# First batch's token mixing in plain float32 on unsplit operands, and channel weights split in two chains

## The chip, the cores and the metric

One core of a Trainium2 chip runs the whole kernel: TensorE (PE for its matmuls, PEld for its weight loads), VectorE (DVE), ScalarE (ACT), GpSimd (POOL), SyncE (SP, which issues most of the DMAs), on-chip memory (SBUF), the matmul accumulators (PSUM, eight banks) and device memory. The metric is device microseconds of one execution of the kernel; lower is better. A number of executions of each kernel gives a median; one more was recorded by the hardware profiler, and every duration in this document comes from such a recording.

## The reference

The inputs are q, k and v (8 batches, 8 heads, 576 positions, 64 wide), two weights of a token mixer (`w_tok1` 576x256, `w_tok2` 256x576) and two of a channel mixer (`w_ch1` 512x1536, `w_ch2` 1536x512). The weights are float64 in memory. Cut to what matters:

```python
q_d, k_d, v_d = means of q, k, v over groups of 4 positions
out = repeat(softmax_attention(q_d, k_d, v_d), 4) + local_attention(q, k, v, |i - j| < 4)
x = out as (batch, 576, 512)
h = relu(x.T @ w_tok1) @ w_tok2          # token mixing, over positions
u = x + h.T
h2 = relu(u @ w_ch1) @ w_ch2             # channel mixing, over the 512 channels
return u + h2
```

## The kernel before, in words

**Batches.** Each of the 8 batches b goes through attention, token mixing (`mix`), and channel mixing (`first`, `second`). Attention works in four head pairs (`pooled`, four steps over the pooled positions: sd, td, ad and their softmax) and five position tiles t of 128, 128, 128, 128 and 64 rows (`local`: scores sc, softmax on DVE and ACT, transpose pT, its copy pt on ACT, product av, copy to x on ACT at L536; the last tile's x is named x_last).

**Token mixing.** `splits` makes two rounded parts of each x tile, a float32r copy on ACT (L570) and the remainder on DVE (L572), in a tile xh. `products` multiplies them, for five tiles into one accumulator named t1 (in the profile it is "t<-xh,W"); each product is `mm3` (L116): three float32r matmuls, high by high, high by low, low by high. `takes` makes relu of it in the same two parts (ACT L607, DVE L609, tile hid), for each of two halves f in turn. Then eight groups t2, for two position chunks (256 and 320 columns) and four channel blocks c: transposes of x through an identity (L595) and two `mm3` with hid ("t<-W,hid"). `takes` copies each group to u (ACT L620) and takes its largest absolute value (DVE L622). `scaled` brings the largest value of a chunk to all partitions (`everywhere`: DVE L544, PE L547, DVE L550, PE L553), and makes uh, u scaled in two float16 parts (ACT L639, DVE L641).

**Channel mixing.** `first` is 12 blocks f for each chunk, each 12 float16 matmuls on uh and the first weight (in the profile "c<-uh,CW"), followed by relu in two parts (L725, L727). `second` is 12 matmuls for each quarter of its sum, on h and the second weight ("c<-h,CX").

**Weights.** Each weight piece comes as float64 words, and `to_f32` makes float32 of it in three steps: ACT (L203), POOL (L206), DVE (L208). The nine token pieces (five of W1, four of W2, tiles W_raw) are then split into two float32r parts by `token_weight`: ACT L226, DVE L228. The channel weights C1 and C2 (12 tiles of 128x512 each) get column norms on PE (L293, L312), a scale, one for each four tiles of C1 and one for all of C2, and a split into two float16 parts by `parts`: ACT L280, DVE L282. The parts of tile i are written over place i, and its float32 lies in place i+1, so tile i+1 can be split only after tile i. `scale` does this in one generator, so the 12 splits run one after the other.

**Order of work.** Each piece of work is a generator that yields `step(engine, estimated us, needs, take, give)`. Until the first batch's channel mixing is through, `drive` plays these estimates as a clock per engine, and issues the step that can start first; among those of the same engine within 0.15 us of it, the one whose generator stands first in the list goes first. The list is a string of group letters, `"LWUMTSaCDPHmQAh"`: loads L, token weights W, up-steps U, mixing of batch 0 M, C2's scale and splits T, C1's scale and splits S, attention of batch 1 a, conversion of C1 C and of C2 D, c1 and c2 products P and Q, the load of batch 1 H, its mixing m, attention of batch 0 A, batch 2's load h. What `drive` chooses is fixed when the program is made; on the chip every engine runs its queue in that order and waits at each instruction for what it needs. Where the estimate leaves PE idle before the first batch's scaled values, `keep_busy` puts matmuls on a tile of ones (L153, "busy<-junk"). After that the remaining work is laid into the channel products of batches 1 to 7 by `side` and `tick`, not by `drive`.

Of the kernel before, what the change touches and what calls it, by code (L numbers as in the profile page):

```python
# [29 lines left out]
PATIENCE = 0.15  # L30
ORDER = """p0+p1 p0 p1 p0 p1 l0+l1 l0 l1 p0 p0 p1 p1 l0 l1 l0 l1 p0 p0 p1 p1 l0 l0 l1 l1
# [5 lines left out]
def tile_ups_attention_mixer(ctx, tc, qk, vw, vr, w1, w2, c1, c2, out):  # L37
# [182 lines left out]
    def token_weight(i, n, f):  # L220
        yield step("A", 0.0, ("W", "raw", i))
        raw = made["W", "raw"][i]
        yield from to_f32(raw, made["W", "raw", i])
        y = raw.rearrange("p (n two) -> p n two", two=2)[:, :, 0].bitcast(F32)
        yield step("A", 0.1 + n * 0.0011)
        nc.scalar.copy(f[:, 0], y)  # L226
        e = yield step("V", 0.08 + n * 0.0012)
        nc.vector.tensor_tensor(f[:, 1], y, f[:, 0].bitcast(F32), ALU.subtract)  # L228
        make(("W", "y", i), e)
        make(("W", "read", i), e)  # L230

# [12 lines left out]
    class Channel:  # L244
# [3 lines left out]
        def __init__(self, name):  # L248
            self.name, self.fin, self.banks = name, [], {}
            self.mx = sb.tile([128, NQ], F32, name=f"{name}_mx")  # L250
            self.inv = [sb.tile([128, 1], F32, name=f"{name}_inv{q}") for q in range(NQ)]
            self.s = [sb.tile([128, 1], F32, name=f"{name}_s{q}") for q in range(NQ)]

        def tile(self, i, *needs):
            name = self.name
            yield step("A", 0.0, (name, "raw", i))
            raw = made[name, "raw"][i]
            e = yield from to_f32(raw, made[name, "raw", i], lambda: self.place[i + 1].bitcast(U32), *needs)
# [3 lines left out]
            self.sums(i, self.place[i + 1].bitcast(BF16).rearrange("p (n two) -> p n two", two=2)[:, :, 1])  # L262
# [13 lines left out]
        def parts(self, i):  # L276
            y = self.place[i + 1]
            f = self.place[i].bitcast(F16).rearrange("p (a n) -> p a n", a=2)
            yield step("A", 0.72)
            nc.scalar.activation(f[:, 0], y, AF.Copy, scale=self.s[i // 4])  # L280
            t = yield step("V", 0.75)
            nc.vector.scalar_tensor_tensor(f[:, 1], y, self.s[i // 4], f[:, 0], ALU.mult, ALU.subtract)  # L282
            self.fin.append(f)
            make((self.name, i), t)

    class First(Channel):
# [8 lines left out]
        def scale(self):  # L295
            for q in range(NQ):
                yield from self.norms(q)
                big = yield from everywhere(f"C1_n{q}", self.mx[:, q:q + 1])
                e = yield step("V", 0.45, give="g")

                self.root(big, 2.0 ** (4.5 + 0.5 - 8), self.inv[q], self.s[q])
                make(("C1", "scale", q), e)
                for i in range(4 * q, 4 * q + 4):
                    yield from self.parts(i)

    class Second(Channel):
# [8 lines left out]
        def scale(self):  # L315
# [5 lines left out]
            yield step("V", 0.9, give="g")  # L321
# [4 lines left out]
            for i in range(NF):  # L326
                yield from self.parts(i)
# [18 lines left out]
    C1.place = singles(NF + 1, "CW")  # L346
# [7 lines left out]
    W2 = [sb.tile([128, 2, S], F32R, name=f"W2_{k}") for k in range(2)]  # L354
    W1_PIECES = [(u32(w1[s0:s0 + n]), 256) for s0, n in TILES]
# [200 lines left out]
    def mix(st):  # L556
# [8 lines left out]
        def splits():  # L565
            for t in range(NT):
# [8 lines left out]
        def products():  # L575
            for t in range(NT):
                e = yield step("P", 1.5, ("W", "y", t), ("xh", b, t), take="" if t else f"gg>{b}")
                if t == 0:
                    st.acc = P2(f"t1_{b}")
                for f in range(2):  # L580
                    mm3(st.acc[:, f], lambda a: W1[t][:, a, 128 * f:128 * f + 128], lambda a: st.xh[t][:, a],
                        t == 0, t == NT - 1)
                make(("t1", b, t), e)
            for ch in range(2):
                s0, N = CHUNKS[ch]
                for c in range(4):
                    e = yield step("P", 1.2, ("W", "y", NT + 3), ("hid", b),
# [15 lines left out]
        def takes():  # L603
            for f in range(2):
# [7 lines left out]
            for ch in range(2):  # L612
# [3 lines left out]
                for c in range(4):  # L616
                    yield step("A", 0.4, ("t2", b, ch, c))
# [87 lines left out]
    def first(st, ch, places):  # L705
        b, N = st.b, CHUNKS[ch][1]
        hs = st.h[ch] = []
        for f in range(NF):
            e = yield step("P", 12 * N * 0.43e-3, ("C1", f), ("uh", b, ch),
                           *([("mixed", b)] if places[f // 3] != "h" else []), take=f"m>1{ch}")  # L710
            uh = st.uh[ch]
            ps = PM(f"c1_{b}_{ch}_{f}")[:, :N]
            for c in range(4):
                mm3(ps, lambda a: C1.fin[f][:, a, 128 * c:128 * c + 128], lambda a: uh[c][:, a], c == 0, c == 3)
# [54 lines left out]
    def second_weights():  # L769
        yield step("S", 0.0, *(("C1", "read", i) for i in range(NF)))  # L770
        C2.place = pairs("CX") + singles(1, "CY")
# [24 lines left out]
    with tc.manual_schedule():  # L796
# [14 lines left out]
        group["T"] = [second_weights()]  # L811
# [7 lines left out]
        streams = [x for k in "LWUMTSaCDPHmQAh" for x in group[k]]  # L819
        left = drive(streams, [("over", 0, 1)] + [("uh", 1, 0)] * (B > 1))  # L820
# [107 lines left out]
```

## Time and profile before

| | |
|---|---|
| median of 3 runs | 945.24 us (937.5 to 946.85) |
| the profiled execution, its own time | 938.98 us |
| its span, first to last instruction | 937.1 us |
| mean granted TensorE clock | 0.985 |
| TensorE in it | 11407 matmul instructions |
| DMA | 68.29 MB, mean 73 GB/s |

Times in the views are us from the span's start. A row of the timeline has start, duration, engine, line, operation, output<-inputs, shape, count, and in brackets the idle time before it with the one it waited for. A row of the groups has the same, then the busy time in all and the mean of one in ns, then idle time before. "t<-xh,W", "t<-W,hid" are the token products; "c<-uh,CW" and "c<-h,CX" the channel products. A busy PE also counts the matmuls on ones.

### The profile page before, as it was taken

Reading aid. Unit: us, or ns where it says so; the run is one execution under the profiler, and the core shown is the slowest. Engines: PE = TensorE matmul, PEld = TensorE weight load, DVE = VectorE, ACT = ScalarE, POOL = GpSimd, SP = SyncE. Lnnn points to the kernel's source line nnn. Section 1 sums busy time; section 2 is a strip of 40 time slices with the busy share of each in tenths; the row PEclk is TensorE's granted clock in tenths of the full one; section 3 lists DMA queues with packets and bytes.
Section 4 is the critical chain, followed back from the end, with each engine's and each line's share of the span. In section 5 each row is a group of like instructions: output and inputs, shape, how many; then the busy total and the mean of one; then the engine's idle time right before and its main releaser. Section 6 shows DMA issues by size and latency. Waiting matters only on the chain.

```text
span 937.1 us, 25758 instructions
## 1 busy us (share of the span) xinstructions
PE 894.0 (95%) x11407; PEld 709.8 (76%) x11413; DVE 482.5 (51%) x1174; ACT 297.7 (32%) x627; POOL 117.0 (12%) x191
## 2 busy tenths in 40 slices
PE   6779998999999999999989999999999999999998
PEld 3556877778867787787867788777977878777876
DVE  6788995437552565327552375426653275333221
ACT  2476553124141332314232241423323142422120
POOL 6350410120310003000130002200030000000000
PEclk9888999999999999999999999999999999999999
DMA  8772432510440006300170004400062000000000
GB/s 238 251 290 99 145 65 66 162 53 2 132 121 8 23 4 191 60 15 16 49 203 3 22 9 145 108 8 23 2 198 54 16 16 20 20 1 29 13 12 29
DMA packets 28222, 68.29 MB, mean 73 GB/s; under 512 B 3504, under 2 KB 14000, under 8 KB 26864
## 3 DMA queue, kind: packets, MB, share of 16 engines
q1 hardware_dynamic: 25552, 64.30, 23.2%
q10 hardware_dynamic: 2560, 2.36, 0.9%
q8 instruction: 89, 1.46, 0.7%
q14 instruction: 21, 0.17, 0.1%
HBM read 54.85 MB, written 9.44 MB: 69 GB/s over the span
## 4 chain that ended last, share of the span: by engine, by line
PE 72%; DMA 5%; DVE 3%; ACT 2%; issue 1%; SPq 0%; ACTq 0%
PE c L116 50%; PE t L116 10%; DMA qk<-in_qk_dram 4%; PE ad L463 3%; PE sc L495 2%; PE t L595 2%; PE av L531 1%; PE sd L436 1%; PE td L454 1%; DMA vw<-od 1%; PE pT L518 1%; ACT x L536 1%; DVE uh L641 1%; PE um_b L553 0%; SPq L371 0%
## 5 line engine op out<-in xcount | busy, mean ns | idle before, releaser
L116 PE MATMUL c<-uh,CW 128*128 128x256 f16 (+1 forms) x2304 | 306.4, 287 | 2.3 <-DVE u L753 1.8
L116 PE MATMUL c<-h,CX 128*128 128x256 f16 (+1 forms) x2304 | 304.5, 287 | 0.1
L116 PEld LDWEIGHTS <-CW 128*128 128x128 f16 x2304 | 219.0, 98 | 68.6 <-issue 14.7
L116 PEld LDWEIGHTS <-CX 128*128 128x128 f16 x2304 | 218.1, 98 | 58.2 <-issue 1.6
L727 DVE SCALAR_TENSOR_TENSOR h<-c,h 128x256 f16<-128x256 f32 (+1 forms) x192 | 86.7, 452 | 135.0 <-ACT h L725 134.9
L725 ACT ACTIVATE h<-c 128x256 f16<-128x256 f32 (+1 forms) x192 | 77.7, 406 | 181.4 <-PE c L116 178.3
L400 POOL TENSOR_TENSOR vr<-vr 72x256 f32<-72x256 f32 x64 | 53.0, 830 | 496.0 <-DMA vr<-in_vr_dram 494.5
L753 DVE SCALAR_TENSOR_TENSOR u<-c,io,u 128x256 f32<-128x256 f32 (+1 forms) x64 | 32.9, 514 | 100.0 <-PE c L116 100.0
L622 DVE TENSOR_REDUCE umx<-t 128x1 f32<-128x256 f32 (+1 forms) x64 | 29.2, 457 | 84.7 <-ACT u L620 76.2
L116 PE MATMUL t<-xh,W 128*128 128x512 f32 x240 | 68.9, 423 | 1.2 <-ACT x L536 1.2
L620 ACT COPY u<-t 128x256 f32<-128x256 f32 (+1 forms) x64 | 25.5, 398 | 133.3 <-PE t L116 110.5
L116 PE MATMUL t<-W,hid 128*128 128x256 f32 (+1 forms) x384 | 66.7, 308 | 0.0
L116 PEld LDWEIGHTS t<-W,hid 128*128 128x128 f32 x384 | 53.2, 189 | 0.3 <-DVE hid L609 0.3
L536 ACT COPY x<-av 128x512 f32<-128x512 f32 x32 | 18.6, 583 | 109.6 <-PE av L531 38.1
L116 PEld LDWEIGHTS t<-xh,W 128*128 128x128 f32 x240 | 44.1, 194 | 11.4 <-ACT x L536 2.0
L463 PE MATMUL ad<-vd,ptd 72*72 72x65 f32 x512 | 39.0, 229 | 7.5 <-issue 6.6
L463 PEld LDWEIGHTS ad<-vd,ptd 72*72 72x72 f32 x512 | 37.3, 146 | 8.9 <-issue 7.6
L531 PE MATMUL av<-vw,pt 47*32 47x64 f32 x2304 | 34.0, 228 | 9.5 <-DMA vw<-od 5.8
L531 PEld LDWEIGHTS av<-vw,pt 47*32 47x32 f32 x2304 | 27.7, 107 | 18.2 <-issue 5.8
L422 DVE TENSOR_REDUCE qd<-qk 128x72 f32<-128x288 f32 x64 | 25.9, 446 | 27.7 <-DMA qk<-in_qk_dram 27.6
L639 ACT ACTIVATE uh<-u,us 128x256 f16<-128x256 f32 (+1 forms) x64 | 29.7, 524 | 26.9 <-DVE us L122 19.8
L495 PEld LDWEIGHTS sc<-qk 64*32 64x32 f32 x2304 | 23.8, 105 | 12.2 <-issue 10.0
(108 smaller groups left out, 841.4 us busy)
## 6 DMA issues: line engine op xcount, KB each, us to landing
qk<-in_qk_dram SPq DMA_DIRECT2D x32, 579.0 KB
vw<-in_vw_dram SPq DMA_DIRECT2D x32, 351.0 KB
vr<-in_vr_dram SPq DMA_DIRECT2D x64, 144.0 KB
C_raw<-in_c_dram SPq DMA_DIRECT2D x16, 512.0 KB
out_dram<-u SPq DMA_DIRECT2D x32, 160.0 KB
C_raws<-in_c_dram SPq DMA_DIRECT2D x8, 512.0 KB
out_dram<-u SPq DMA_DIRECT2D x32, 128.0 KB
vw<-od ACTq DMA_DIRECT2D x32, 72.0 KB
```

Of the source, the lines that this page charges most:

```text
L116: nc.tensor.matmul(ps, lhs(a), rhs(c), start=first and i == 0, stop=last and i == 2, **kw)
L400: nc.gpsimd.tensor_add(t[:, 0:2], t[:, 0:2], t[:, 2:4])
L422: nc.vector.tensor_reduce(o, q[:, h], axis=AX.X, op=ALU.add)
L463: nc.tensor.matmul(ps[:, g, par], pt[:, par, kg, G * g:G * g + G], st.vd[:, kg, 2 * pr + par], start=kg == 0, stop=kg == 1)
L495: nc.tensor.matmul(ps[QB * j:QB * j + QB, par, WB * hp:WB * hp + WB], st.qk[hp][p, QB * g:QB * g + QB], st.qk[hp][p, S + QB * g:S + QB * g ...
L531: nc.tensor.matmul(ps[QB * j:QB * j + QB, par, D * hp:D * hp + D], pt[p, hp, QB * j:QB * j + QB], st.vw[h][p, g, D * hp:D * hp + D], start ...
L536: nc.scalar.copy(x[:n].rearrange("p hp two d -> p two hp d"), ps[:n, :, :4 * D].rearrange("p two (hp d) -> p two hp d", hp=4))
L622: nc.vector.tensor_reduce(umx[ch][:, c:c + 1], ps, axis=AX.X, op=ALU.max, apply_absolute_value=True)
L639: nc.scalar.activation(t[:, 0], st.u[ch][c], AF.Copy, scale=s)
L725: nc.scalar.activation(ht[:, 0], ps, AF.Relu)
L727: nc.vector.scalar_tensor_tensor(ht[:, 1], ps, 0.0, ht[:, 0], ALU.max, ALU.subtract)
L753: nc.vector.scalar_tensor_tensor(us[c], banks[c], io, us[c], ALU.mult, ALU.add)
```

## The change

For batch 0 alone, the token products take x, W1, relu and W2 unsplit, in plain float32: one `matmul` call in place of the three of `mm3`. `splits` runs from batch 1 on, and `takes` of batch 0 has the two ACT relus and no DVE step. The float32 of W1 goes to a tile of its own in the u1 buffers (W1_y), that of W2 to a new tile W2_y. The two-part split of the nine pieces, which batches 1 to 7 use, is a generator `token_split` in a new group w, next to last in the list; it needs the first batch's t1 product of that tile (W1) or all of its token products (W2). A copy of batch 0's u waits for the first of these splits, and one of batch 1's for all five of W1, since u1 is shared.

The float32 of C1 and C2 now lies two places up (i+2), so the splits go in two chains, even and odd tiles, in generators of their own (`split(0)`, `split(1)`; group E for C1, in T for C2). The planner's list becomes `"LWUMSETaCDPHmQAwh"`: S and E stand before T. The planner's estimate of a t1 tile of batch 0 is 1.8 instead of 1.5 us.

```diff
+PRIORITY = "LWUMSETaCDPHmQAwh"
...
     def token_weight(i, n, f):
...
-        yield from to_f32(raw, made["W", "raw", i])
-        y = raw.rearrange("p (n two) -> p n two", two=2)[:, :, 0].bitcast(F32)
-        yield step("A", 0.1 + n * 0.0011)
-        nc.scalar.copy(f[:, 0], y)
-        e = yield step("V", 0.08 + n * 0.0012)
-        nc.vector.tensor_tensor(f[:, 1], y, f[:, 0].bitcast(F32), ALU.subtract)
+        if i < len(TILES):
+            y = WY[i] = T([f.shape[0], n], F32, "u1", f"W1_y{i}")
+        else:
+            y = WY[i]
+        e = yield from to_f32(raw, made["W", "raw", i], lambda: u32(y))
         make(("W", "y", i), e)
         make(("W", "read", i), e)
+
+    def token_split(i, n, f):
+        yield step("A", 0.1 + n * 0.0011, ("W", "y", i), ("t1", 0, i) if i < len(TILES) else ("mixed", 0))
+        nc.scalar.copy(f[:, 0], WY[i])
+        e = yield step("V", 0.08 + n * 0.0012)
+        nc.vector.tensor_tensor(f[:, 1], WY[i], f[:, 0].bitcast(F32), ALU.subtract)
+        make(("W", "split", i), e)
...
         def parts(self, i):
-            y = self.place[i + 1]
+            y = self.place[i + 2]
...
-                for i in range(4 * q, 4 * q + 4):
-                    yield from self.parts(i)
+
+        def split(self, k):
+            for i in range(k, NF, 2):
+                yield step("A", 0.0, ("C1", "scale", i // 4))
+                yield from self.parts(i)
...
-            for i in range(NF):
+            make(("C2", "scale"), made["S2"])
+
+        def split(self, k):
+            yield step("A", 0.0, ("C2", "scale"))
+            for i in range(k, NF, 2):
                 yield from self.parts(i)
...
-            for t in range(NT):
+            for t in range(NT if b else 0):
                 yield step("A", 0.62, ("x", b, t), *([("over", 0, 0)] if b == 1 else []),
...
-                    mm3(st.acc[:, f], lambda a: W1[t][:, a, 128 * f:128 * f + 128], lambda a: st.xh[t][:, a],
-                        t == 0, t == NT - 1)
+                    if b == 0:
+                        n = TILES[t][1]
+                        nc.tensor.matmul(st.acc[:, f], WY[t][:, 128 * f:128 * f + 128], xf(t)[:n],
+                                         start=t == 0, stop=t == NT - 1)
+                    else:
+                        mm3(st.acc[:, f], lambda a: W1[t][:, a, 128 * f:128 * f + 128], lambda a: st.xh[t][:, a],
+                            t == 0, t == NT - 1)
...
-                        mm3(ps, lambda a: st.hid[k][:, a, 128 * c:128 * c + 128],
-                            lambda a: W2[k][:, a, s0:s0 + N], False, k == 1, skip_group_check=True)
+                        if b == 0:
+                            nc.tensor.matmul(ps, st.hid[k][:, 128 * c:128 * c + 128], W2_y[:, k, s0:s0 + N],
+                                             start=False, stop=k == 1, skip_group_check=True)
+                        else:
+                            mm3(ps, lambda a: st.hid[k][:, a, 128 * c:128 * c + 128],
+                                lambda a: W2[k][:, a, s0:s0 + N], False, k == 1, skip_group_check=True)
...
+            if b == 0:
+                ht = T([128, 2, 512], F32, "xh", "hid0")
+                for f in range(2):
+                    e = yield step("A", 0.6, ("t1", 0, NT - 1), give="gg>0" if f else "")
+                    nc.scalar.activation(ht[:, f], st.acc[:, f], AF.Relu)
+                    st.hid.append(ht[:, f])
+            for f in range(2 if b else 0):
...
+                    yield step("A", 0.4, ("t2", b, ch, c), *[("W", "split", i) for i in range(NT if b else 1) if b < 2 and ch and c == (0 if b else 3)])
...
+        group["w"] = [token_split(i, pieces[i][1], fin[i]) for i in range(len(pieces))]
+        group["E"] = [C1.split(k) for k in range(2)]
+        group["T"] = [second_weights(), C2.split(0), C2.split(1)]
```

More of the change, by code (lines that the diff above doesn't have):

```diff
@@ L248, in __init__ @@
         def __init__(self, name):
-            self.name, self.fin, self.banks = name, [], {}
+            self.name, self.fin, self.banks = name, {}, {}
             self.mx = sb.tile([128, NQ], F32, name=f"{name}_mx")
@@ L257, in tile @@
             raw = made[name, "raw"][i]
-            e = yield from to_f32(raw, made[name, "raw", i], lambda: self.place[i + 1].bitcast(U32), *needs)
+            e = yield from to_f32(raw, made[name, "raw", i], lambda: self.place[i + 2].bitcast(U32), *needs)
             make((name, "read", i), e)
@@ L261, in tile @@
             make((name, "y", i), e)
-            self.sums(i, self.place[i + 1].bitcast(BF16).rearrange("p (n two) -> p n two", two=2)[:, :, 1])
+            self.sums(i, self.place[i + 2].bitcast(BF16).rearrange("p (n two) -> p n two", two=2)[:, :, 1])
         def norms(self, q):
@@ L282, in parts @@
             nc.vector.scalar_tensor_tensor(f[:, 1], y, self.s[i // 4], f[:, 0], ALU.mult, ALU.subtract)
-            self.fin.append(f)
+            self.fin[i] = f
             make((self.name, i), t)
@@ L320, in scale @@
             big = yield from everywhere("C2_n", self.mx)
-            yield step("V", 0.9, give="g")
+            made["S2"] = yield step("V", 0.9, give="g")
             self.root(big, 2.0 ** (4.5 + 2 + 0.5 - 14), ic, self.s[0])
@@ L345, in tile_ups_attention_mixer @@
     C1, C2 = First("C1"), Second("C2")
-    C1.place = singles(NF + 1, "CW")
+    C1.place = singles(NF + 2, "CW")
     ic = sb.tile([128, 1], F32, name="ic")
@@ L354, in tile_ups_attention_mixer @@
     W2 = [sb.tile([128, 2, S], F32R, name=f"W2_{k}") for k in range(2)]
+    W2_y = sb.tile([128, 2, S], F32, name="W2_y")
+    WY = {len(TILES) + 2 * k + j: W2_y[:, k, HS * j:HS * j + HS] for k in range(2) for j in range(2)}
     W1_PIECES = [(u32(w1[s0:s0 + n]), 256) for s0, n in TILES]
@@ L576, in products @@
             for t in range(NT):
-                e = yield step("P", 1.5, ("W", "y", t), ("xh", b, t), take="" if t else f"gg>{b}")
+                e = yield step("P", 1.5 if b else 1.8, *([("W", "split", t), ("xh", b, t)] if b else [("W", "y", t), ("x", 0, t)]),
+                               take="" if t else f"gg>{b}")
                 if t == 0:
@@ L586, in products @@
                 for c in range(4):
-                    e = yield step("P", 1.2, ("W", "y", NT + 3), ("hid", b),
+                    e = yield step("P", 1.2, *(("W", "split" if b else "y", NT + i) for i in range(4)), ("hid", b),
                                    *([("over", b - 1, 0)] if b and ch == 0 else []), take="" if c % 2 else f"gg>{b}")
@@ L603, in takes @@
         def takes():
-            for f in range(2):
+            if b == 0:
[5 more added lines that the diff above has]
+            for f in range(2 if b else 0):
                 yield step("A", 0.6, ("t1", b, NT - 1))
@@ L770, in second_weights @@
         yield step("S", 0.0, *(("C1", "read", i) for i in range(NF)))
-        C2.place = pairs("CX") + singles(1, "CY")
+        C2.place = pairs("CX") + singles(2, "CY")
         make(("C2", "places"), now[0])
@@ L818, in tile_ups_attention_mixer @@
         group["h"] = [lazily(lambda: ahead(2), ("x", 1, last))]
-        streams = [x for k in "LWUMTSaCDPHmQAh" for x in group[k]]
-        left = drive(streams, [("over", 0, 1)] + [("uh", 1, 0)] * (B > 1))
+        streams = [x for k in PRIORITY for x in group[k]]
+        left = drive(streams, [("over", 0, 1), ("C1", NF - 1)] + [("uh", 1, 0)] * (B > 1))
     def rest(items):
```

5 lines of the change are left out of this document (1 added, 4 removed).

## The prediction

> **What bounds the kernel now.** I read the page first, then the busy time by stretches, then the timeline of the three engines up to the first channel product. On the page TensorE is the busiest engine:
>
> ```profile
> span 937.1 us, 25758 instructions
> ...
> PE 894.0 (95%) x11407; PEld 709.8 (76%) x11413; DVE 482.5 (51%) x1174; ACT 297.7 (32%) x627; POOL 117.0 (12%) x191
> ```
>
> The stretches say where that does and does not hold (busy time of PE, weight loads, DVE, ACT, POOL, then clock and DMA share):
>
> ```profile
> 0.00:90.00 90.00, 68.67 (x964) 46.08 (x971) 69.23 (x162) 46.90 (x90) 38.27 (x68) 0.89 0.68 215
> 90.00:145.00 55.00, 53.39 (x755) 43.41 (x754) 51.18 (x126) 27.68 (x55) 14.89 (x22) 0.97 0.39 112
> 145.00:200.00 55.00, 52.45 (x641) 41.11 (x640) 21.51 (x44) 13.17 (x25) 7.53 (x12) 0.97 0.37 110
> 200.00:937.00 737.00, 719.44 (x9054) 579.23 (x9052) 340.62 (x844) 209.91 (x457) 56.36 (x89) 1.00 0.18 50
> ```
>
> From 90 us on PE is idle for 1.6, 2.6 and 17.6 us of 55, 55 and 737: the rest of the kernel is PE's own queue, and what starts it earlier ends it earlier. Before 90 us PE has 21.3 us without work and part of the rest is matmuls on ones:
>
> ```profile
> L153 PE MATMUL busy<-junk 128*128 128x512 bf16 x67 | 21.2, 439 | 2.8 <-DVE junk L86 1.6 <-issue 0.4 <-DVE C_n_m L550 0.3
> ```
>
> So the change can act on the time up to the first channel product. That point, and the last step before it, are rows of PE and DVE:
>
> ```profile
> 60.53 0.65 PE L531 MATMUL av<-vw,pt 47*32 47x64 f32 x32
> ...
> 66.35 0.61 PE L293 MATMUL C_sum<-CW 128*128 128x128 bf16 x4 [3.10 <-DVE CW L208]
> ...
> 68.38 3.18 PE L116 MATMUL t<-xh,W 128*128 128x512 f32 x6
> ...
> 74.28 0.95 PE L116 MATMUL t<-W,hid 128*128 128x256 f32 x6
> ...
> 77.05 0.95 PE L116 MATMUL t<-W,hid 128*128 128x256 f32 x6
> ...
> 83.59 0.38 PE L553 MATMUL um_b<-um_m,ones 1*128 1x1 f32 x2
> ...
> 90.18 2.76 PE L116 MATMUL c<-uh,CW 128*128 128x256 f16 x12
> ...
> 104.36 3.11 PE L116 MATMUL c<-uh,CW 128*128 128x256 f16 x24
> ```
>
> ```profile
> 67.88 1.13 DVE L572 TENSOR_TENSOR xh<-x_last,xh 128x512 fp32r<-128x512 f32 x1
> ...
> 73.63 0.67 DVE L609 SCALAR_TENSOR_TENSOR hid<-t,hid 128x512 fp32r<-128x512 f32 x1
> ...
> 89.68 0.48 DVE L641 SCALAR_TENSOR_TENSOR uh<-u,us,uh 128x256 f16<-128x256 f32 x1
> ...
> 100.72 0.55 DVE L641 SCALAR_TENSOR_TENSOR uh<-u,us,uh 128x320 f16<-128x320 f32 x1
> ```
>
> The product at 90.18 needs the last uh (89.68 + 0.48 = 90.16). Going back: uh comes from the largest value, which PE spreads at 83.59 behind the token groups; those start at 74.28 behind the last half of hid on DVE (73.63); that follows the last t1 product (68.38 to 71.56); and that waits for the last tile x, through ACT:
>
> ```profile
> 65.54 0.56 ACT L536 COPY x_last<-av 64x512 f32<-64x512 f32 x1
> 66.14 0.62 ACT L570 CAST xh<-x_last 128x512 fp32r<-128x512 f32 x1
> ...
> 71.60 0.60 ACT L607 ACTIVATE hid<-t 128x512 fp32r<-128x512 f32 x1 [2.37 <-PE t L116]
> 72.09 0.67 ACT L203 ACTIVATE C_raw<-C_raw 128x512 f32<-128x512 f32 x1
> 72.95 0.60 ACT L607 ACTIVATE hid<-t 128x512 fp32r<-128x512 f32 x1 [0.19 <-DVE hid L609]
> ...
> 79.51 0.35 ACT L620 COPY u<-t 128x256 f32<-128x256 f32 x1
> ```
>
> The product av of this tile was through at 61.18 (60.53 + 0.65), yet ACT copied it only at 65.54: 4.4 us in ACT's queue, where attention of batch 0 stands low in the list. This is the path that the change shortens.
>
> **The change part by part.** Price of a plain float32 product first, since the trace of before has none of this size. Rows of the chain, each the time that PE needs from one to the next:
>
> ```profile
> 174.52 1.40 PE t L116 x6
> ...
> 191.33 0.22 PE t L595 x2
> 191.54 0.71 PE t L116 x6
> ...
> 201.95 0.90 PE t L116 x6
> ...
> 223.92 1.03 PE ad L463 x16
> ```
>
> The float32r product takes 1.40/6 = 0.233 us for 512 columns, 0.71/6 = 0.118 for 256, 0.90/6 = 0.150 for 320 (0.45 to 0.47 ns a column). The pooled product ad is plain float32; its loop calls 8 matmuls and the row counts 16, so a call shows as two instructions, each 1.03/16 = 0.064 us for 65 columns, 0.99 ns a column. The float32 transposes take 0.22/2 = 0.11 us for 128 columns, 0.86 ns. So I take 0.86 to 0.99 ns a column for each of two instructions: 0.88 to 1.01 us for 512 columns against 3 x 0.233 = 0.70. Bounds: from below two instructions at the float32r rate, 0.46 us; from above 1.01 us at half clock, 2.0 us. I take the middle of the two nearest rows, 0.95. On PE that is 10 x 0.25 = 2.5 us more for t1, and for t2 8 x 0.12 and 8 x 0.14, 2 us more, mostly in place of matmuls on ones.
>
> *Term A, last x to end of t1.* Before: 66.10 (65.54 + 0.56) to 71.56, 5.46 us, of which ACT's cast, DVE's remainder and six slow matmuls. After: two plain products, 1.8 to 2.0 us at full clock. The clock there was low:
>
> ```profile
> 68.00:72.00 4.00, 3.99 (x11) 2.27 (x11) 3.45 (x5) 1.63 (x4) 2.92 (x4) 0.50 0.37 146
> ```
>
> At 0.50 they take 3.5 to 4.0. I take 2.5, a gain of 3.0 (1.4 to 3.7). The Trainium skill, TensorE: Matmul & The Clock Gate, section What's actually happening, has a rule that speaks against counting on the full clock: after an idle window of about 3.4 us TensorE drops to half, and comes back only after as long a busy one. The trace agrees so far: the 0.50 follows a gap of 3.10 us ahead of the row at 66.35. By the rule, if the gap stays, term A gains 1.7 and the sum below is 5.2; if the copy comes close behind av, 3.6 and 7.1.
>
> *Term B, hid.* Before 71.60 to 74.28, 2.7 us, ACT and DVE in turn. After, two ACT relus of 0.60, 1.2, or 1.9 with one other 0.67 between. I take 1.5: gain 1.2 (0.8 to 1.5).
>
> *Term C, t2.* A group of chunk 0 grows from 0.71 to 0.88 to 1.01, four of them 0.7 to 1.2; a group of chunk 1 from 0.90 to 1.10 to 1.27, and the spread at 83.59 stands behind up to four of these. Part is covered: the last group of chunk 0 ended at 78.00, and ACT took it at 79.51. Loss 1.0 (0, if all is covered, to 2.7).
>
> *Term D, ACT's and DVE's queue ahead of the last x.* What stands there from the stretch 41 to 65.5 us:
>
> ```profile
> L572 DVE TENSOR_TENSOR xh<-x,xh 128x512 fp32r<-128x512 f32 x4 | 3.4, 851 | 0.2 <-ACT xh L570 0.2
> L228 DVE TENSOR_TENSOR W<-W_raw,W 128x288 fp32r<-128x288 f32 (+2 forms) x7 | 3.2, 469 | 2.0 <-ACT W L226 1.9
> ...
> L226 ACT CAST W<-W_raw 128x288 fp32r<-128x288 f32 (+2 forms) x7 | 3.0, 446 | 7.5 <-DMA vw<-od 4.6 <-DVE W_raw L208 2.8
> ...
> L570 ACT CAST xh<-x 128x512 fp32r<-128x512 f32 x4 | 2.5, 624 | 0.1
> ...
> L280 ACT ACTIVATE CW<-CW,C_s 128x512 f16<-128x512 f32 x3 | 2.2, 723 | 0.0
> ```
>
> The change takes 3.0 + 2.5 = 5.5 us from ACT and 3.2 + 3.4 = 6.6 from DVE here. How much reaches the copy is to be read from how full both are, with the later stretch beside it:
>
> ```profile
> 41.00:65.50 24.50, 18.34 (x363) 12.84 (x363) 20.52 (x44) 18.18 (x37) 11.14 (x12) 0.91 0.79 278
> 90.18:155.10 64.92, 60.76 (x1003) 48.88 (x1007) 57.50 (x138) 33.95 (x67) 14.89 (x22) 0.97 0.35 98
> ```
>
> Of 24.5 us DVE is busy 20.5 and ACT 18.2: three quarters to five sixths. The moved splits of W1 come last in the list and may use the holes, a chance that each costs its 0.45. Against it, the new chains of C1 splits stand ahead of the copy, two of 0.72 us at a time where there was one. I take 4.0 less 0.7, 3.3. Bounds: 6.6, all of DVE's removed work; and a loss of 3.6, if eight splits stand ahead of the copy instead of the three in the row of L280 (5 x 0.72).
>
> *After 90 us.* The four W2 splits, and what of W1 is left, are up to 9 x 0.45 = 4.0 us of DVE and ACT each; DVE has 64.9 - 57.5 = 7.4 us free up to 155, which hides them. If that cover were gone, they would delay the C2 splits by 4.0. Two chains for C2 shorten a stretch that was serial:
>
> ```profile
> 124.72 0.72 ACT L280 ACTIVATE CX<-CX,C_s 128x512 f16<-128x512 f32 x1 [1.99 <-DVE C_s L325]
> ```
>
> ```profile
> 154.26 0.75 DVE L282 SCALAR_TENSOR_TENSOR CX<-CY,C_s,CX 128x512 f16<-128x512 f32 x1 [0.92 <-ACT CX L280]
> ```
>
> Twelve splits in 30.3 us, 2.5 each, for 0.74 of DVE. PE has other work meanwhile, so I give it nothing; bounds a gain of 2 (of the 2.6 idle in 145 to 200) and a loss of 4. The new waits: the fourth copy of u in chunk 1 waits for the first W1 split, and behind it in that generator stand uh of chunk 1 (last at 100.72) and chunk 1's first product, which lies in the row at 104.36. That is some 3 us of cover; later than that, it costs one for one. Batch 1's copies wait for splits that may start after t1 (71.56), and that batch's first group of chunk 1 is the chain's row at 201.95. On SP's queue nothing moves back: the token pieces free their raw buffers two steps earlier, so the channel loads behind them come no later. The new order of groups I hold at nothing; the bounds above cover it.
>
> *Sum.* -3.0 - 1.2 + 1.0 - 3.3 = -6.5 us at the first channel product (near 83.7), carried to the end by PE's queue. The profiled execution had 938.98; that makes 932.5. It lay 6.26 us below the median of the runs, 945.24; taken from the median, 938.7.
>
> **The rivals.**
>
> *The freed slots all reach the path.* Attention of batch 0 is starved by work that goes away, and DVE is the fuller engine. With D at 6.6, A at 3.5, B at 1.5 and C at 0.7 the gain is 10.9: 928.1 on the profiled execution, 934.3 on the median. For it: the wait of 4.4 us in ACT's queue. Against: the conversions of C1 stand higher in the list and take slots first.
>
> *The head start is not kept.* Channel products start 6.5 us earlier, but the moved splits, 4.0 us, go into DVE's queue ahead of C2's, and PE ends up waiting for C2: gain 2.5 or less, 936.5, median 942.7. For it: DVE is busy 57.5 of 64.9 us there. Against: those splits stand low in the list, and two chains hurry C2.
>
> *Slower: the C1 chains crowd out attention.* Both chains keep ACT and DVE filled at once, and both stand ahead of the first batch's attention. If eight or more splits precede the copy of the last x, D becomes +3.6; with A and B at their low ends, -1.4 - 0.8, C at 1.7, the sum is +3.1: 942.1, median 948.3. It decides from about seven splits on ahead of the copy, where D takes up what A and B give. For it: the list. Against: the step that can start first goes first, and the list settles only ties within 0.15 us; the scale that the splits of C1 need is itself made behind the same queue.
>
> **How the numbers follow.** Forecast 0.48, freed slots 0.24, head start lost 0.16, slower 0.12. The predicted time is the forecast's, 938.7. The runs shown differ by 1.0% among themselves, so 1%, 9.4 us, is about what a measurement of this kernel can tell from no change. The range reaches to the second case less some 4 us of that scatter, 930, and up to the slower case, 948. Faster by over 1%: most of the freed-slots case and a tenth of the forecast, 0.26. Slower by over 1%: the tail of the slower case and of the plain float32 price at its upper bound, 0.07. Within 1%: 0.67. The likeliest case by itself runs from 935 to 943.
>
> **What would show it.** Right: the plain products as two instructions each, 20 for t1 at 0.86 to 0.99 ns a column where the clock is full; no xh or hid remainder on DVE before the first "c<-uh,CW"; that product at 82 to 86 us; the copy of x_last within 2 us of the end of its av; idle PE after it no more than before. A first channel product at 80 or earlier is the second case; one near 84 with more idle PE between 100 and 160 the third; eight or more "CW<-CW" on ACT before x_last and a first channel product after 90 the fourth. The prediction is wrong in its mechanism if the first channel product moves and the end does not, or the other way round.

## The result, and the profile after

The changed kernel takes 933.92 us (median of 13 runs, 932.24 to 940.04), the kernel before 944.5 (13 runs, 937.5 to 949.68). The medians differ by 10.6 us, the means by 8.2 (935.4 and 943.6). The ratio, 0.9913 with a 95% interval of 0.9884 to 0.9943, goes with the means: 8.2 us less (5.4 to 11.0), clear of zero and a little under the 1% that was called the limit of what can be told. Forecast were 6.5 us less and 938.7. The two profiled executions, which the readings below compare, differ by 5.8 us (933.15 and 938.98). In the ratios of the experiments below, executions that took over 1.5% longer than the fastest of their kernel are left out, among them one of e2 with 1274.4 us, one of e5 with 1022.6 and one of the kernel before with 1028.5.

The page after, its first lines, and the same stretches as before:

```profile
span 931.3 us, 25674 instructions
...
PE 892.4 (96%) x11371; PEld 704.3 (76%) x11376; DVE 477.1 (51%) x1167; ACT 294.1 (32%) x622; POOL 112.2 (12%) x191
```

```profile
0.00:90.00 90.00, 72.42 (x968) 45.99 (x974) 65.88 (x159) 43.67 (x88) 34.86 (x68) 0.89 0.68 221
90.00:145.00 55.00, 53.46 (x757) 42.73 (x756) 53.15 (x126) 29.70 (x58) 14.20 (x22) 1.00 0.34 102
145.00:200.00 55.00, 51.89 (x642) 41.24 (x641) 20.70 (x49) 11.72 (x23) 8.27 (x14) 1.00 0.38 114
200.00:931.00 731.00, 714.68 (x9011) 574.37 (x9009) 337.34 (x836) 209.03 (x453) 54.88 (x87) 1.00 0.18 50
```

PE is idle for 1.5, 3.1 and 16.3 us in the last three stretches, much as before (1.6, 2.6, 17.6): the rest of the kernel is again PE's queue. The path to the first channel product, on PE and ACT of the changed kernel:

```profile
59.36 0.65 PE L547 MATMUL av<-vw,pt 47*32 47x64 f32 x32
...
60.71 1.98 PE L600 MATMUL t<-x_last,W_y 64*128 64x512 f32 x4
62.62 0.63 PE L300 MATMUL C_sum<-CW 128*128 128x128 bf16 x8
...
63.96 1.17 PE L621 MATMUL t<-W_y,hid 128*128 128x256 f32 x4
...
74.16 0.27 PE L563 MATMUL um_t<-ident,um_m 128*1 128x128 f32 x1
...
75.77 0.38 PE L569 MATMUL um_b<-um_m,ones 1*128 1x1 f32 x2
...
83.13 2.49 PE L117 MATMUL c<-uh,CW 128*128 128x256 f16 x12
```

```profile
60.08 0.58 ACT L552 COPY x_last<-av 64x512 f32<-64x512 f32 x1 [0.33 <-PE av L547]
...
62.73 0.60 ACT L634 ACTIVATE hid<-t 128x512 f32<-128x512 f32 x1 [0.17 <-PE t L600]
...
63.79 0.58 ACT L634 ACTIVATE hid<-t 128x512 f32<-128x512 f32 x1
...
77.74 0.43 ACT L652 COPY u<-t 128x320 f32<-128x320 f32 x1 [1.80 <-PE t L621]
78.06 0.51 ACT L671 ACTIVATE uh<-u,us 128x256 f16<-128x256 f32 x1
```

```profile
76.56 0.16 DVE L123 RECIPROCAL us<-ui 128x1 f32<-128x1 f32 x1
```

The copy of the last x (60.08) now starts 0.07 us after its av is through (59.36 + 0.65), where it waited 4.36. There is no split between it and t1 (60.71), none between hid (62.73, 63.79) and t2 (63.96). The first channel product starts at 83.13, 7.05 us earlier; the forecast had 83.7. Its first group takes 2.49 us, where the next takes 1.47: PE had stood idle for 2.88 us up to 82.30, and its clock is 0.50 from 82 to 85. The first channel product of batch 1, in both kernels, ahead the changed one:

```profile
200.84 0.39 PE L117 MATMUL c<-uh,CW 128*128 128x256 f16 x2
```

```profile
207.50 0.83 PE L116 MATMUL c<-uh,CW 128*128 128x256 f16 x6
```

Of the 7.05 us 6.66 are still there at this point, 5.8 at the end of the span.

### The profile page after: what moved, and what is told of

Read it like the earlier page. It is cut to its first block, busy times and chain, and to the rows that moved or that the text cites. A ratio compares the mean times of both kernels' runs of the same rounds, so it can differ in the third digit from the quotient of the medians.

```text
span 931.3 us, 25674 instructions
## 1 busy us (share of the span) xinstructions
PE 892.4 (96%) x11371; PEld 704.3 (76%) x11376; DVE 477.1 (51%) x1167; ACT 294.1 (32%) x622; POOL 112.2 (12%) x191
## 4 chain that ended last, share of the span: by engine, by line
PE 81%; DVE 7%; DMA 7%; ACT 3%; issue 2%; SPq 0%; ACTq 0%; POOL 0%; DVEq 0%; POOLq 0%
PE c L117 53%; PE t L117 10%; PE ad L479 3%; DMA qk<-in_qk_dram 3%; PE sc L511 2%; PE av L547 2%; PE sd L452 2%; PE t L617 2%; DMA vw<-od 2%; PE pT L534 2%; PE td L470 1%; PE busy L154 1%; DMA out_dram<-u 1%; DVE uh L673 1%; DMA C_raw<-in_c_dram 1%
## 5 line engine op out<-in xcount | busy, mean ns | idle before, releaser
L416 POOL TENSOR_TENSOR vr<-vr 72x256 f32<-72x256 f32 x64 | 51.1, 801 | 488.7 <-DMA vr<-in_vr_dram 453.7
L117 PE MATMUL t<-xh,W 128*128 128x512 f32 x210 | 58.3, 413 | 1.2 <-ACT x L552 1.2
L117 PE MATMUL t<-W,hid 128*128 128x256 f32 (+1 forms) x336 | 58.5, 308 | 0.0
L117 PEld LDWEIGHTS t<-W,hid 128*128 128x128 f32 x336 | 46.6, 189 | 0.3 <-DVE hid L641 0.3
L117 PEld LDWEIGHTS t<-xh,W 128*128 128x128 f32 x210 | 37.6, 189 | 9.4 <-ACT x L552 1.8
L417 POOL TENSOR_TENSOR vd<-vr 72x128 f32<-72x128 f32 x64 | 33.1, 523 | 4.0
```

Of the source, the lines that this page charges most:

```text
L117: nc.tensor.matmul(ps, lhs(a), rhs(c), start=first and i == 0, stop=last and i == 2, **kw)
L416: nc.gpsimd.tensor_add(t[:, 0:2], t[:, 0:2], t[:, 2:4])
L417: nc.gpsimd.tensor_add(st.vd[:, g, 2 * pr:2 * pr + 2, :D], t[:, 0].rearrange("p (h d) -> p h d", d=D), t[:, 1].rearrange("p (h d) -> p h d ...
```

## The experiments

Twelve kernels were run, ten of them 6 to 12 times, e6 and e7 in one profiled execution each. There is one profile of each. The numbers that answer most questions are landmarks of each profile (us from the span's start): the copy of the last x, the first t2 product, the first uh step on ACT, the first channel product c1, the distance from there to batch 1's first channel product, and the span. The ratio is to the kernel before.

| kernel | copy | t2 | uh | c1 | to batch 1's c1 | span | ratio (95%) |
|---|---|---|---|---|---|---|---|
| before | 65.54 | 74.28 | 85.13 | 90.18 | 117.3 | 937.1 | |
| changed | 60.08 | 63.96 | 78.06 | 83.13 | 117.7 | 931.3 | 0.9913 (0.9884 to 0.9943) |
| e1_plain | 60.93 | 65.73 | 80.30 | 85.48 | 121.2 | 938.5 | 0.9942 (0.9912 to 0.9972) |
| e2_chains | 63.38 | 72.81 | 84.00 | 89.70 | 119.8 | 937.9 | 0.9998 (0.9962 to 1.0034) |
| e3_wearly | 61.08 | 64.93 | 81.41 | 85.47 | 117.3 | 934.5 | 0.9964 (0.9927 to 1.0001) |
| e4_est | 60.60 | 64.48 | 77.95 | 82.53 | 120.6 | 932.5 | 0.9924 (0.9891 to 0.9957) |
| e5_t1only | 61.79 | 68.91 | 84.48 | 88.90 | 120.6 | 941.4 | 1.0013 (0.9974 to 1.0053) |
| e6_t2half | 60.46 | 64.34 | 75.92 | 80.62 | 114.7 | 928.6 | one run |
| e7_t2twice | 60.50 | 64.39 | 85.45 | 90.53 | 115.3 | 936.0 | one run |
| e8_xhback | 59.15 | 63.01 | 77.00 | 81.71 | 117.4 | 929.6 | 0.9946 (0.9910 to 0.9982) |
| e9_order | 61.08 | 64.97 | 75.69 | 80.79 | 124.7 | 935.7 | 0.9975 (0.9943 to 1.0006) |
| e10_afirst | 52.20 | 69.26 | 81.45 | 86.27 | 133.0 | 948.8 | 1.0103 (1.0039 to 1.0168) |
| e11_late | 60.69 | 64.36 | 78.58 | 82.75 | 117.4 | 931.0 | 0.9933 (0.9895 to 0.9971) |
| e12_both | 59.75 | 63.41 | 74.46 | 79.56 | 127.9 | 937.3 | 0.9974 (0.9927 to 1.0020) |

From batch 1's first channel product to the end all fourteen take 728.4 to 733.3 us. So a time is c1, plus the sixth column, plus some 730. How far one profile can be read: e6, e7 and e9 have ACT's queue up to the copy in the same order as the changed kernel, and their copies still lie 0.4 to 1.0 us later.

### Which part makes the gain: e1_plain and e2_chains

e1_plain keeps the plain mixing and the later weight splits, with one chain and the old places:

```diff
-PRIORITY = "LWUMSETaCDPHmQAwh"
+PRIORITY = "LWUMTSaCDPHmQAwh"
...
-            y = self.place[i + 2]
+            y = self.place[i + 1]
...
-        group["E"] = [C1.split(k) for k in range(2)]
...
-        group["T"] = [second_weights(), C2.split(0), C2.split(1)]
+        group["T"] = [second_weights()]
```

> Plain float32 mixing of the first batch and its later weight splits, but the channel weights split in one chain each and the groups S and E as before. Theory: the gain is that of the mixing path (last x copied earlier, no split between x and t1, none between hid and t2), so most of it is here: first channel product at 82 to 86 us, ratio to the kernel before 0.991 to 0.996. Rival (the two chains and the new order of groups make the gain): first channel product at 88 or later, ratio 0.997 to 1.000.

e2_chains is the reverse: the kernel before with the two chains and the new order of groups alone.

```diff
...
+        group["E"] = [C1.split(k) for k in range(2)]
...
-        group["T"] = [second_weights()]
+        group["T"] = [second_weights(), C2.split(0), C2.split(1)]
...
-        streams = [x for k in "LWUMTSaCDPHmQAh" for x in group[k]]
+        streams = [x for k in "LWUMSETaCDPHmQAh" for x in group[k]]
```

> Only the two chains of channel weight splits and the new order of groups; the first batch's mixing as before. Theory: little for the first channel product, 88 to 91 us against 90.2, ratio 0.997 to 1.002; the C2 splits end some 5 us earlier than 155 without moving the end. Rival: the chains make the gain, ratio 0.991 to 0.995.

The first channel products of e1 and of e2:

```profile
85.48 1.47 PE L117 MATMUL c<-uh,CW 128*128 128x256 f16 x12
```

```profile
89.70 1.47 PE L116 MATMUL c<-uh,CW 128*128 128x256 f16 x12
```

The plain mixing alone brings c1 forward by 4.7 us and the runs by 0.6%; the chains alone by 0.5 us and nothing that can be measured. The gain is that of the mixing path, as in the theory, though not all of it was seen to be kept: in e1's profile batch 1's first channel product is only 0.8 us earlier than before, since 121.2 us pass to it instead of 117.3. In e2 the C2 splits end at 140.8 us instead of 155.0, some 14 us earlier and not the 5 that were expected, and the end does not move. Together the parts bring 7.05 us, more than 4.7 + 0.5, but the intervals of 0.9942 and 0.9913 overlap, so that the chains add anything to the time is not shown. In e2 the copy comes 2.2 us earlier than before although no work was taken away: a first sign that its place is a matter of order.

### What brought the copy of the last x forward: e3_wearly, e8_xhback, e10_afirst

Three runs put work back or change the order alone. e3 puts the splits of W back where they were:

```diff
-PRIORITY = "LWUMSETaCDPHmQAwh"
+PRIORITY = "LWwUMSETaCDPHmQAh"
...
-        yield step("A", 0.1 + n * 0.0011, ("W", "y", i), ("t1", 0, i) if i < len(TILES) else ("mixed", 0))
+        yield step("A", 0.1 + n * 0.0011, ("W", "y", i))
```

> The changed kernel, but the two-part splits of the nine token weight pieces stand again right behind their conversion in the list and wait for nothing else. Theory: part of the earlier copy of the last x comes from these splits being out of its way, 7 of them of 0.45 us on ACT and DVE: the copy 1 to 3 us later than at 60.1, first channel product at 84 to 86, ratio 0.993 to 0.997 to the kernel before. Rival (they lie in holes of ACT and DVE wherever they stand): first channel product within 1 us of 83.1, ratio 0.990 to 0.993.

e8 puts the splits of the first batch's x back, with nothing that reads them:

```diff
-            for t in range(NT if b else 0):
+            for t in range(NT):
                 yield step("A", 0.62, ("x", b, t), *([("over", 0, 0)] if b == 1 else []),
```

> The changed kernel, but the five x tiles of the first batch are split again into xh, which nothing reads: the work is back in ACT's and DVE's queues, the dependence on it is not. Theory (the earlier copy of the last x is queue relief): five times 0.62 us on ACT and 0.7 to 1.1 on DVE push the copy to 62 to 63.5 us, first channel product at 84.5 to 86.5, ratio to the kernel before 0.993 to 0.997. Rival (only the dependence counted): the copy within 0.6 us of 60.1, first channel product within 1 us of 83.1, ratio 0.990 to 0.993.

```profile
59.15 0.56 ACT L552 COPY x_last<-av 64x512 f32<-64x512 f32 x1
```

```profile
81.71 1.47 PE L117 MATMUL c<-uh,CW 128*128 128x256 f16 x12
```

With the splits in ACT's and DVE's queues again, four of them ahead of the copy, it came 0.9 us earlier than without them, not 2 to 3 later, and c1 at 81.7. The theory of queue relief is not borne out for this work; what is left as its part is that t1 no longer waits for it. In e3 the copy is 1.0 us later and c1 2.3, within what was expected. But e9, whose order on ACT up to the copy is that of the changed kernel, has the copy at 61.08 as well, so that the W splits hold it up is not shown; what grew in e3 is the way from t2 to uh (16.48 us against 14.10). e10 is the kernel before, with attention of the first batch further up in the list and nothing else:

```diff
-        streams = [x for k in "LWUMTSaCDPHmQAh" for x in group[k]]
+        streams = [x for k in "LAWUMTSaCDPHmQh" for x in group[k]]
```

> The kernel before with one change: attention of the first batch stands second in the planner's list instead of last but one. Theory (the last x was copied late because of its place in ACT's queue, not because ACT had no time): the copy within 1.5 us of the end of its av, at 60 to 62.5 us instead of 65.5; the split, hid and their waits stay, so first channel product at 86 to 88.5, ratio 0.994 to 0.999. Rival (ACT and DVE are simply full, only less work helps): the copy at 64 or later, first channel product at 89 or later, ratio 0.998 to 1.003.

The last av, its copy on ACT, and a later stretch:

```profile
51.05 1.07 PE L531 MATMUL av<-vw,pt 47*32 47x64 f32 x32
```

```profile
52.20 0.58 ACT L536 COPY x_last<-av 64x512 f32<-64x512 f32 x1 [0.16 <-PE av L531]
```

```profile
140.00:160.00 20.00, 13.72 (x230) 11.02 (x229) 12.11 (x27) 8.46 (x15) 0.12 (x1) 0.61 0.41 136
```

The copy comes at 52.20, 13.3 us earlier, with all the work of before. That is further than expected, because the whole attention moved: 9.1 us come from its av, through at 52.12 instead of 61.18, and 4.3 from the wait behind it, now 0.08 us. So the copy's place was set by the list, and ACT had the time. It is paid elsewhere: the split of this x came on DVE only at 62.09, c1 at 86.27, and then 133 us pass to batch 1's c1 instead of 117, with PE at a clock of 0.61 between 140 and 160. The kernel is 1.0% slower. My range of 0.994 to 0.999 was wrong, because I looked at c1 alone.

### What the plain products cost on the path: e6_t2half and e7_t2twice

e6 leaves the second half of hid out of the first batch's t2 products, e7 issues each of them twice into the same sum; the order of every queue stays. So neither computes the whole result.

```diff
-                    for k in range(2):
+                    for k in range(2 if b else 1):
...
```

```diff
-                    for k in range(2):
+                    for k in range(2 if b else 4):
...
```

> The changed kernel with half of the first batch's t2 products left out (the second half of hid); the order of every queue stays. In the changed kernel it is 14.1 us from the first t2 product (63.96) to the first uh step on ACT (78.06), against 10.9 before. Theory (the price of plain products is on this path): a group is 0.5 to 0.6 us shorter, four of chunk 0 and two or three of chunk 1 stand ahead, so 10.5 to 12 us there, first channel product at 79.5 to 81. Rival (ACT and DVE set the pace of copies and maxima): 13 to 14.1 us, first channel product at 82.2 to 83.1.

> The changed kernel with each of the first batch's t2 products issued twice into the same sum (so that sum counts the hidden values twice); the order of every queue stays. Theory (price on the path): four groups of chunk 0 grow by 1.0 each and three of chunk 1 by 1.2, so 7.8 us more from the first t2 product to the first uh step, 21 to 22 us, first channel product at 90 to 91. Rival (cover by ACT and DVE): 4 to 6 us more, first channel product at 87 to 89.

First uh step and first channel product, ahead with half of them, then with twice:

```profile
75.92 0.51 ACT L671 ACTIVATE uh<-u,us 128x256 f16<-128x256 f32 x1
```

```profile
80.62 1.47 PE L117 MATMUL c<-uh,CW 128*128 128x256 f16 x12
```

```profile
85.45 0.51 ACT L671 ACTIVATE uh<-u,us 128x256 f16<-128x256 f32 x1
```

```profile
90.53 1.70 PE L117 MATMUL c<-uh,CW 128*128 128x256 f16 x7
```

From the first t2 product to the first uh step it is 11.58 us with one plain product (two instructions) in each group, 14.10 with two, 21.06 with four: 2.5 to 3.5 us for each further product in all groups, in both runs as the theory had it. The price of the products is on the path, with little cover.

### Plain float32 in t1 alone: e5_t1only

```diff
...
-                        if b == 0:
-                            nc.tensor.matmul(ps, st.hid[k][:, 128 * c:128 * c + 128], W2_y[:, k, s0:s0 + N],
-                                             start=False, stop=k == 1, skip_group_check=True)
-                        else:
-                            mm3(ps, lambda a: st.hid[k][:, a, 128 * c:128 * c + 128],
...
+                        mm3(ps, lambda a: st.hid[k][:, a, 128 * c:128 * c + 128],
...
-            for f in range(2 if b else 0):
+            for f in range(2):
...
+        group["W"] += [token_split(i, pieces[i][1], fin[i]) for i in range(len(TILES), len(pieces))]
```

> The changed kernel with plain float32 in t1 alone: hid and W2 are split again and t2 is three float32r products, the four W2 splits stand right behind their conversion. Theory (a plain t2 costs about as much on this path as it saves at hid): from the first t2 product to the first uh step 11 to 12.5 us instead of 14.1, hid 1.0 to 1.5 us longer, W2 splits again ahead; first channel product at 82 to 84.5, ratio to the kernel before 0.990 to 0.995. Rival (plain t2 is a loss that t1's gain hides): first channel product at 80 to 81.5, ratio 0.986 to 0.990.

```profile
64.50 0.59 ACT L629 ACTIVATE hid<-t 128x512 fp32r<-128x512 f32 x1
...
67.31 0.60 ACT L629 ACTIVATE hid<-t 128x512 fp32r<-128x512 f32 x1 [0.80 <-DVE hid L631]
```

```profile
60.00:80.00 20.00, 16.24 (x116) 11.46 (x116) 15.86 (x30) 12.81 (x27) 7.67 (x9) 0.83 0.48 193
```

Neither came true: c1 at 88.9 and no gain at all. hid with its split takes from 64.50 to t2 at 68.91, 4.4 us instead of 1.2. In that time PE stands idle for 2.0 us, and behind it the clock is at half from 70 to 76 us (0.83 over the stretch). t2's groups then take 15.6 us to the first uh step, although their products are cheaper; in the kernel before, with the same three products at full clock, it was 10.85. So the way through hid was worth more here than its own 1.5 us. That the clock is the cause is likely by these rows, but no run takes it apart from the W2 splits that stand earlier again.

### Can more be had: e4_est, e9_order, e11_late, e12_both

e4 gives the planner a truer price of a t2 group of chunk 1:

```diff
-                    e = yield step("P", 1.2, *(("W", "split" if b else "y", NT + i) for i in range(4)), ("hid", b),
+                    e = yield step("P", 1.2 if b or not ch else 1.5, *(("W", "split" if b else "y", NT + i) for i in range(4)), ("hid", b),
```

> The changed kernel with one planner's estimate changed: a chunk 1 group of the first batch's t2 counts 1.5 us instead of 1.2, about what the trace shows (1.50 from one to the next). Theory: uh's first ACT step stood behind a copy of u that was planned too early (1.80 us of ACT waiting at 77.74); with the true price it goes first, first channel product at 81.5 to 82.5, ratio 0.989 to 0.992. Rival: the order of the whole stage shifts with any edit, and the first channel product lands anywhere from 81 to 86.

c1 came at 82.53 (2.77 us for its first group, with the clock at 0.54 from 82 to 84), but the wait of uh behind the copy of u stayed (78.06 became 77.95): a truer estimate did not bring the uh step ahead, and the reason given was wrong. The time is that of the changed kernel. e9 lets the last three groups of chunk 1 wait until chunk 0's scale is known, and puts the uh steps ahead of the copies of u in the list:

```diff
-                                   *([("over", b - 1, 0)] if b and ch == 0 else []), take="" if c % 2 else f"gg>{b}")
+                                   *([("over", b - 1, 0)] if b and ch == 0 else []), *([("us", 0)] if not b and ch and c else []), take="" if c % 2 else f"gg>{b}")
...
+                make(("us", b), now[0])
...
-        return [splits(), products(), takes(), scaled()]
+        return [splits(), products(), takes(), scaled()] if b else [products(), scaled(), takes()]
```

> A version meant to go beyond the changed kernel: of the first batch's t2 groups the last three of chunk 1 wait until chunk 0's largest value is known, and the uh steps stand ahead of the u copies in the list. Theory: the spread on PE and the first uh step on ACT no longer stand behind chunk 1; us known at 74 to 75 us instead of 76.7, first channel product at 79.5 to 81.5, ratio to the kernel before 0.986 to 0.991. Rival: chunk 1's groups come to stand ahead of the first channel product anyway or delay uh of chunk 1, first channel product at 82 to 84, ratio 0.991 to 0.995.

The first uh step now follows its scale at once (75.65 to 75.69), and c1 is 2.3 us earlier than in the changed kernel, as expected; the time is 0.9975, not 0.986 to 0.991. What PE waited for between 100 and 160 us, the step in question, and what the DMA queues did from 116 to 121.2 us:

```profile
PE sc L511 <- issue: 4.2, 1, 4.2
PE av L547 <- DMA vw<-od: 2.3, 2, 1.8
```

```profile
121.11 0.50 PE L511 MATMUL sc<-qk 64*32 64x38 f32 x28 [4.16 <-issue]
```

```profile
q1 hardware_dynamic: 121, 0.86, 78.2%
q8 instruction: 1, 0.02, 1.9%
```

PE stood for 4.2 us at a score product of batch 1 with nothing in the profile to wait for ("issue"); in that time 78% of the DMA engines' time went to the loads of batch 1, and one packet of 16 KB came for the instruction queue. Behind it the clock is 0.51 from 121 to 128 us. Two further runs ask whether DVE's load there is the cause instead. e11 is the changed kernel with later splits of W, e12 is e9 with the same:

```diff
-        yield step("A", 0.1 + n * 0.0011, ("W", "y", i), ("t1", 0, i) if i < len(TILES) else ("mixed", 0))
+        yield step("A", 0.1 + n * 0.0011, ("W", "y", i), ("t1", 0, 0) if i == 0 else ("c1", 0, 1, NF - 1) if i < len(TILES) else ("over", 0, 0))
```

> The changed kernel with later weight splits: W1's second to fifth wait until the last c1 product of the first batch, W2's until its first half is over; DVE is half idle there. Theory (between 83 and 145 us DVE, 95 to 97% busy, holds PE up): some 3.5 us of DVE work leave that stretch, first channel product at 81.5 to 83, ratio to the kernel before 0.986 to 0.990. Rival (DVE's load there holds nothing up): ratio 0.990 to 0.994.

> The later weight splits together with the changed order of chunk 1's t2 groups, whose first channel product was at 80.8 with no gain at the end. Theory (that head start was lost to DVE's load and comes through when DVE has room): first channel product at 79.5 to 81, ratio to the kernel before 0.984 to 0.989. Rival (it was lost to a wait of PE for its own instructions under load of the transfers, 4.2 us and a drop of the clock behind it): ratio 0.991 to 0.998, with a wait of PE on issue of over 2 us between 100 and 160.

DVE's stretches of e11, then of the changed kernel:

```profile
100.00:120.00 20.00, 19.26 (x296) 15.30 (x297) 18.46 (x38) 8.96 (x19) 12.08 (x19) 1.00 0.62 176
120.00:140.00 20.00, 18.51 (x283) 14.30 (x282) 19.32 (x53) 13.13 (x25) 0.00 (x0) 1.00 0.01 2
```

```profile
100.00:120.00 20.00, 19.67 (x350) 15.09 (x348) 19.31 (x44) 9.27 (x20) 12.25 (x19) 1.00 0.66 178
120.00:140.00 20.00, 19.31 (x181) 15.24 (x182) 19.18 (x47) 13.26 (x24) 0.00 (x0) 1.00 0.01 2
```

e11 gains nothing on the changed kernel (0.9933 and 0.9913, overlapping): DVE is as full as before (18.5 and 19.3 of 20 us, against 19.3 and 19.2), so the room that the theory asked for was not made. That DVE holds PE up is thus not confirmed, and not excluded either. e12 came out as its rival said:

```profile
79.56 1.38 PE L117 MATMUL c<-uh,CW 128*128 128x256 f16 x10
```

```profile
PE sc L511 <- issue: 4.9, 1, 4.9
PE av L547 <- DMA vw<-od: 2.2, 2, 1.6
```

The earliest c1 of all kernels, 79.56, and a time of 0.9974: the same wait on issue, 4.9 us (117.6 to 122.5), stands again between c1 and batch 1. It does not settle DVE's part, since DVE was as full there as in e9 (19.0 and 19.7 of 20 us from 100 to 120).

Whether PE waited for instructions that came late behind the loads was not tried. For it: in e9 and in e12 the packet of the instruction queue comes some 3 us ahead of PE's next product, inside the gap. Against it as the whole account: in e12 the loads took only 39% of the DMA engines' time in the gap, and nothing moved in its last microsecond; and in the changed kernel PE stood for 1.7 us on issue at 149.9 with no transfer at all, a packet of that queue having come at 149.0 to 149.5. The queue has 89 packets in the span, and others come without any such wait. So the wait is seen, and its cause is open. No kernel here beats the changed one beyond its interval.

## Why the prediction was right, and where it was not

**The path and its landmark.** That the change acts on the time up to the first channel product, and that PE's queue carries this to the end, held for this kernel: -7.05 there against -6.5, and -6.66 at batch 1's. It is no rule: in e1, e9 and e12 most or all of a head start was gone by then. The profiled pair shows 5.8 at the end. The runs show 8.2, and the profiled execution of the kernel before, 938.98, lies low among its 13 runs (937.5 to 949.7). Within one kernel the time goes loosely with the granted clock: of the changed kernel's 13 runs the shortest span, 930.4 us, had 0.994 and the longest, 938.0, had 0.985, but 931.7 was also seen at 0.987.

**The price of a plain product** was right, near enough. In the chain of the changed kernel four instructions of 256 and of 320 columns take:

```profile
66.03 0.87 PE t L621 x4
...
73.24 1.08 PE t L621 x4
```

0.87/4 and 1.08/4 us are 0.85 and 0.84 ns a column, and t1's last tile, 60.71 to 62.62 in four of 512, 0.93; the range was 0.86 to 0.99, so t2's products lie just under it.

**The terms** (us, forecast and measured): A, last x to the end of t1, -3.0 and -3.4 (5.46 became 2.03); B, hid, -1.2 and -1.45 (2.72 became 1.27); C, t2 to uh, +1.0 and +3.25 (10.85 became 14.10); D, the copy, -3.3 and -5.46. C lies beyond its bound of 2.7, D within its bound of 6.6. C is 2.25 us worse than forecast and D 2.16 better, so that the sum came within 0.6 us of its forecast is in part luck.

**Term A** came out at full clock. The stretch 60 to 80 us, before and after:

```profile
60.00:80.00 20.00, 16.19 (x125) 11.41 (x127) 16.55 (x32) 14.27 (x27) 9.18 (x10) 0.83 0.48 195
```

```profile
60.00:80.00 20.00, 17.89 (x96) 11.16 (x96) 16.09 (x36) 14.26 (x30) 6.47 (x8) 1.00 0.43 172
```

Of the two cases weighed there, the copy came close behind av, the gap of 3.1 us was gone, and the case of 3.6 held, near enough. The clock over this stretch went from 0.83 to 1.00. With the Trainium skill's rule (TensorE: Matmul & The Clock Gate, section What's actually happening: half clock after an idle window of about 3.4 us) the trace agrees in kind, but not in the figure: the half clock also followed gaps of 3.10 us in the kernel before and of 2.88 us in the changed one.

**Term C** was sized too small, and three things are seen in it. The products' price was taken as partly covered. e6 and e7 show 2.5 to 3.5 us for each plain product in all groups; one takes 0.435 us for 256 columns against 0.355 for three float32r ones, and 0.54 against 0.45 for 320. So the step from the one to the other, a fifth to a sixth of it, is by estimate 0.8 to 1.3 us for the two products of each group. Then PE stood for copies of u on ACT, 0.35 us at 65.59 and 1.07 at 72.69, where the groups of the kernel before have one wait of 0.31:

```profile
72.69 0.44 PE L617 MATMUL t<-ident,x 128*128 128x128 f32 x2 [1.07 <-ACT u L652]
```

And the uh step, which had followed its scale at once (85.09 to 85.13), stood 1.34 us (76.72 to 78.06) behind a copy of u that waited for a group of chunk 1, which I had not seen. e9 takes that away, and chunk 1 out of the spread's way: from t2 to uh it is then 10.72 us, with the same plain products. How the three add up to the 3.25 is not worked out further.

**Term D** failed in its cause. The prediction read it from how full ACT and DVE are, and from the work that goes away. Of the 5.46 us 1.17 come from an earlier av (61.18 became 60.01) and 4.29 from the wait behind it. e8 puts about half of that work back (the splits of x, not those of W and hid) and the copy is no later; e10 takes nothing away and moves it by 13.3 us, 9.1 of them with its av. What counts is the place in the queues, which the list and its estimates set. Nor was all of the work gone: three of W1's splits still stood ahead of the copy on ACT (46.79, 51.07 and 54.47). Which edit moved it is not settled: e1 without the chains has 60.93, e3 with the early W splits 61.08, e2 without the plain mixing 63.38.

**The rivals.** All freed slots on the path: by the median alone, 933.92, this case (934.3) would have won over the forecast (938.7). Its A and B came, and D fell short of its 6.6 by 1.1; but C was 3.25 and not 0.7, so c1 was at 83.13 and not at 80 or earlier. The medians lie 10.6 us apart, the profiled executions 5.8; what makes the rest is not shown. The head start not kept: not for this kernel, but for e9 and e12, where PE's wait on issue is seen and no wait for C2. The crowding out: two C1 splits stood ahead of the copy on ACT (57.86), not eight.

## What to carry to other kernels

A step taken out of a dependence chain and the same work taken out of a queue are two things, and to put the work back without its reader tells them apart. In a schedule laid out by estimates, a landmark reached earlier is worth something only if the next stage keeps its length: read the time from landmark to landmark, not one landmark alone. Where operands are split only to be multiplied a few times, a plain product that costs a fifth to a third more than its three parts can still win, as long as the matmul engine is not the bound there.

## What the runs showed of the hardware

A plain float32 product here is two instructions of 0.84 to 0.93 ns a column, against 0.45 to 0.47 for one float32r instruction. PE's clock was at half behind idle gaps of 3.10 us (before, from 66 us) and 2.88 us (changed, from 82 us). PE stood with nothing in the profile to wait for, for 4.2 us in e9 while the loads of batch 1 took 78% of the DMA engines' time, and for 4.9 us in e12 while they took 39%. One 16 KB packet of the instruction queue lies in each gap, and one in the wait of 6.6 us at 18 us in the kernel before. And from run to run the changed kernel's span differs by 7.6 us (930.4 to 938.0), loosely with the mean granted clock.
